# Near products over blocks of 16 tokens, split between VectorE and GpSimd, in a recurrent attention with a feed-forward

## The chip, the cores and the metric

The kernel runs on one core of a Trainium2 chip, in one launch. The metric is the device time in microseconds (us) of an execution; the time before is the median of 6 runs. The profiles are of one execution each. The engines are called by their names in the profile: PE (TensorE, matmuls; PEld are its weight loads), DVE (VectorE), ACT (ScalarE), POOL (GpSimd) and SP (SyncE, which here only issues DMAs).

## The reference

A recurrence over 768 tokens for 4 x 8 heads of 48 channels, then a feed-forward over all 3072 tokens with weights of 384 x 2048 and 2048 x 384:

```python
for t in range(S):
    kt, vt, rt, wt = (k[:, :, t], v[:, :, t], r[:, :, t], w[:, :, t])
    cur = np.einsum('bhd,bhe->bhde', u[None] * kt, vt)
    y[:, :, t] = np.einsum('bhd,bhde->bhe', rt, state + cur)
    state = wt[:, :, :, None] * state + np.einsum('bhd,bhe->bhde', kt, vt)
...
h = x @ w_in
sp = np.maximum(h, 0.0) + np.log1p(np.exp(-np.abs(h)))
g = h * erf(sp)
return (g @ w_out).astype(np.float32)
```

For one head, the weight with which token t reads token s before it is the sum over channels of r[t] k[s] times the product of w over the tokens between them; for s = t it is the sum of r u k. All of it is computed in fp32.

## The kernel before

**Steps.** The work is cut into 12 steps, s = 0 to 11. A step is a stretch of 128 tokens for 2 of the 4 batches, that is 16 heads; even steps hold one pair of batches, odd steps the other. The text counts them from one as well: the fifth step is s = 4. Each step has an attention (`attend`, L350) and a feed-forward of 256 tokens in two halves: `hidden` (L520, 8 pieces of 6 matmuls on L547, then softplus, erf and a product, L529, L532, L536) and `project` (L559, 8 pieces of 4 matmuls on L568). While step s runs its attention, the hidden part of step s - 1 and the projection of step s - 3 run as filling between the attention's parts.

**Levels.** Within a half of 64 tokens the weights between tokens are made by doubling. At level l the pairs are those whose blocks of 2^(l-1) tokens are neighbours in one block of 2^l. PE multiplies r with k (L390, 32 matmuls of 64 x 64 into the tile pp, each of two passes, so 64 instructions in the profile), and the part that belongs to the level is taken over into the tile own (copy_predicated with a mask, L409, on DVE; level 6 by a copy on ACT, L416). Before that DVE scales r and k in place by the totals of w (`scale`, L231), so that the next level's products have the decay in them: the matmuls of level l + 1 wait for the scale of level l. The totals, products of w over 2, 4, ... tokens, are made on POOL (L306, six instructions a step, tile tot_sb).

**Near tokens.** From s = 4 on (`DIRECT`), levels 1 to 3 aren't made by PE. The weights within blocks of `NEAR` = 8 tokens are made directly: r, k and w of the step are loaded a second time with tokens as rows (`load_rows`, L150), and for each distance n from 0 to 7 POOL multiplies k by one more w (L295) and by r (L289, L292, L296). DVE sums each over the 48 channels (L324, tile sums), the sums go to memory and come back with another shape (L330, L332, tiles by_blocks and by_tokens), and one product with a block mask (L342) spreads them over own. In these steps PE makes levels 4, 5 and 6.

**Order.** The kernel writes the order of each engine's queue by hand; every engine works through its queue in order. `prepare(s + 1)` (L235) is a generator: the attention of step s takes one stretch of it at a time, by `next(following)` at L420 and after the transposes (L455), and what is left after the states. Its first stretch has the near products and totals. `place(n)` (L654) is called at each level and at two further points; it runs what is due of softplus, erf and product (`advance`) and then pieces of projection or hidden (`beside`). From s = 4 on these are 4, 4, 3, 3 and 2 pieces in the five places. SP's queue has all loads and stores: behind a step come the three transfers into xT (L512), then the loads for the step after next (`load_step`, `load_rows`), the two stores of o (L578), by_blocks and by_tokens.

**Rest of a step.** After the levels: matmuls from own (L435), transposes of k (L446), new states (L464; DVE L476 and L484, POOL L452 and L480), matmuls from the states into y (L498), and y goes over ACT and DMAs into xT, the feed-forward's input. In the first four steps weights are also converted (L187 to L203), and all six levels run on PE.

The line that says when a stretch of the preparation is taken is

```python
            if level > (NEAR_LOG if s >= DIRECT - 1 else 1):
                next(following, None)
            place(level - 1)
```

Of the kernel before, what the change touches and what calls it, by code (L numbers as in the profile page):

```python
# [11 lines left out]
FP32 = mybir.dt.float32  # L12
# [21 lines left out]


DIRECT = 4
NEAR_LOG = 3
NEAR = 1 << NEAR_LOG
LOG = 6
MASKED = 5  # L40
# [2 lines left out]
def view(ap, offset, dims):  # L43

    return bass.AP(ap.tensor, ap.offset + offset, [ap.ap[0], *dims])
# [12 lines left out]
def kernel(  # L58
# [28 lines left out]
    assert n_steps == SPC * n_pairs and NP == KT + 1 == 4 and NG == 2 and P // NEAR * NH // 2 == P  # L87
# [23 lines left out]
    first = const.tile([P, HC], FP32, name="first")  # L111
    block_sb = const.tile([P, HC], FP32, name="block_sb")

    sums = const.tile([P, NEAR, 2, NEAR], FP32, name="sums")
    u_row = const.tile([P, 2 * D], FP32, name="u_row")
# [110 lines left out]
    def scale(s, level):  # L226

        in_t, tots = loaded[s][0], ready[s][1]
        half, nb = 1 << (level - 1), JP * C >> level
        halves = view(in_t[:, 0:2], half, [[JP * C - half, 2], [2 * half, nb], [1, half]])  # L230
        nc.vector.tensor_mul(  # L231
            halves, halves, view(tots[level - 1], 0, [[1, 2], [2, nb], [0, half]])
        )

    def prepare(s):  # L235


        in_t = loaded[s][0]
        if s < DIRECT:
            rk1 = att.tile([P, 2, JP, C], FP32, name="rk1", bufs=1)  # L240
            parts = 1 if s else NJ
            def multiply_u(i, x):
                n = slice(i * JP // parts, (i + 1) * JP // parts)
                with_u, plain = (
                    [
                        t[:, x, n].rearrange("p n (t two) -> p n t two", two=2)[..., one]
                        for t in (rk1, in_t)
                    ]
                    for one in (x, 1 - x)
                )  # L250
# [12 lines left out]
                nc.scalar.copy(plain[0], plain[1])  # L263

            if s < 2:
                for i in range(parts):
                    for x in range(2):
                        multiply_u(i, x)
                yield
            else:  # L270
                yield
                yield
                multiply_u(0, 0)
        if s >= DIRECT:
# [4 lines left out]
            room = [front[:].rearrange("p x n t -> p (x n t)")] + [  # L279
                back[:].rearrange("p x n two -> p (x n two)").bitcast(FP32)  # L280
            ]
            terms = []
            for n in range(NEAR):
                if n in (0, 3):
                    free, used = room.pop(0), 0
                size = (NEAR - n) * 2 * D
                terms.append(free[:, used : used + size].rearrange("p (t n) -> p t n", n=2 * D))
                used += size
            nc.gpsimd.tensor_mul(  # L289
                terms[0], k, u_row[:, None, :].to_broadcast([P, NEAR, 2 * D])  # L290
            )
            nc.gpsimd.tensor_mul(terms[0], terms[0], r)  # L292
            for n in range(1, NEAR):
                if n > 1:
                    nc.gpsimd.tensor_mul(k[:, : NEAR - n], k[:, : NEAR - n], w[:, n - 1 : NEAR - 1])  # L295
                nc.gpsimd.tensor_mul(terms[n], r[:, n:], k[:, : NEAR - n])  # L296

        tots, tot = [], in_t[:, 2].rearrange("p n t -> p (n t)")
        tot_sb = att.tile([P, JP * (C - NC)], FP32, name="tot_sb")
        used = 0  # L300
        for level in range(1, LOG + 1):
            tots.append(tot)
            nb = JP * C >> level
            new = tot_sb[:, used : used + nb]
            pair = tot.rearrange("p (n two) -> p n two", two=2)
            nc.gpsimd.tensor_mul(new, pair[:, :, 0], pair[:, :, 1])  # L306
            tot = new
            used += nb
            if level == 2 and s < DIRECT:
                yield  # L310
        if s < DIRECT:
            ready[s] = rk1, tots, tot
            yield
            if s >= 2:
                yield
                multiply_u(0, 1)
            return

        own = att.tile([P, NH, HC], FP32, name="own")
        ready[s] = own, tots, tot  # L320
        yield
        yield
        for n in range(NEAR):
            nc.vector.tensor_reduce(  # L324
                out=view(sums[:], n, [[2 * NEAR + 1, NEAR - n], [NEAR, 2]]),
                in_=terms[n].rearrange("p t (n d) -> p t n d", d=D),
                axis=mybir.AxisListType.X, op=ALU.add,
            )
        by_blocks = dram.tile([P, NEAR, 2 * NEAR], FP32, name="by_blocks")
        nc.sync.dma_start(out=by_blocks[:], in_=sums[:].rearrange("p s n t -> p s (n t)"))  # L330
        by_tokens = att.tile([P, NH, NEAR], FP32, name="by_tokens", bufs=1)
        nc.sync.dma_start(  # L332
            out=by_tokens[:].rearrange("p (g n) t -> p g (n t)", n=2),
            in_=by_blocks[:].rearrange("(g b) s n -> (b s) g n", g=NH // 2),
        )
# [13 lines left out]

    def attend(s, xT, place, behind):  # L350
# [29 lines left out]
        for level in range(NEAR_LOG + 1 if s >= DIRECT else 1, LOG + 1):  # L380
# [213 lines left out]
    def beside(s, k):  # L594


        kind, of, pieces = (projs, s - 3, 2) if k < 4 else (hids, s - 1, 2)
        if s >= DIRECT:
            kind, of = (projs, s - 3) if k < 2 else (hids, s - 1)
            pieces = (4, 4, 3, 3, 2)[k]  # L600
        if s in ALONE:
            kind, of, pieces = hids, s - 1, 1
        if not 0 <= of < n_steps:
# [3 lines left out]
        for _ in range(pieces):  # L607
            next(kind[of])


    CONVERT = (
# [13 lines left out]
    with tc.manual_schedule(  # L625
# [19 lines left out]
        for s in range(n_steps):  # L645
            xTs[s] = xs.tile([P, KT, UNIT], FP32, name="xT")
            places = iter(range(8))

            def convert_at(n):
                if s < len(CONVERT) and n < len(CONVERT[s]):  # L650
                    for what in CONVERT[s][n]:
                        conversion.send(what)

            def place(n):  # L654
                if s in ALONE:
                    convert_at(n)
                    advance(ALONE[s][n])
                else:
                    advance()
                    convert_at(n)  # L660
                beside(s, next(places))

            attend(s, xTs[s], place, lambda: convert_at(LOG + 2))
            if s + 2 < n_steps:
                load_step(s + 2)
                if s + 2 >= DIRECT:
                    load_rows(s + 2)
        for k in range(15):
            advance()
            beside(n_steps + k // 5, k % 5)  # L670


def level_masks():
# [94 lines left out]
```

## Time and profile before

| | |
|---|---|
| median of 6 runs | 637.38 us (637.2 to 638.08) |
| the profiled execution | 637.2 us, of it 635.4 us span |
| granted PE clock | 1.000 |
| DVE, L231, scales, 72 of 128 x 1024 | 100.9 us busy |
| DVE, L536, h products, 48 of 128 x 1024 | 80.1 us busy, 1708 ns each |
| DVE, L324, reduces, 64 of 16 down to 2 sums | 38.2 us busy |
| POOL, L289 to L296, near products, 120 | 134.4 us busy |
| POOL, L306, totals, 72 | 66.8 us busy |

Busy time is what the instructions of a group took from start to end, so it has in it what an instruction lost to others after it had started. An engine's idle time costs nothing by itself; it does where the engine is the one that the end waits for. In rows of a timeline the first number is the start in the span, the second the time from the first start to the last end of a run of equal instructions, and a bracket at the end is the idle time before it and who ended it.

How the twelve steps lie: the fourth step (s = 3) goes from 105.7 to 158.4 us, the eight late steps (s = 4 to 11) follow at 48.8 us each until 549.2 us, and then the last projections run until the end.

### The profile page before, as it was taken

Reading aid. Unit: us, or ns where it says so; the run is one execution under the profiler, and the core shown is the slowest. Engines: PE = TensorE matmul, PEld = TensorE weight load, DVE = VectorE, ACT = ScalarE, POOL = GpSimd, SP = SyncE. Lnnn points to the kernel's source line nnn. Section 1 sums busy time; section 2 is a strip of 40 time slices with the busy share of each in tenths; the row PEclk is TensorE's granted clock in tenths of the full one; section 3 lists DMA queues with packets and bytes.
Section 4 is the critical chain, followed back from the end, with each engine's and each line's share of the span. In section 5 each row is a group of like instructions: output and inputs, shape, how many; then the busy total and the mean of one; then the engine's idle time right before and its main releaser. Section 6 shows DMA issues by size and latency. Waiting matters only on the chain.

```text
span 635.4 us, 16193 instructions
## 1 busy us (share of the span) xinstructions
PE 622.4 (98%) x7338; PEld 458.2 (72%) x7338; DVE 307.6 (48%) x311; ACT 301.1 (47%) x374; POOL 276.0 (43%) x240
## 2 busy tenths in 40 slices
PE   8889999999999999999999999999999999999997
PEld 7567787678678678668668668768768758768654
DVE  4588597577336276266265365366446322011110
ACT  2537778756424544544534524624614625634520
POOL 4338175495195196097097087088079100000000
PEclk9999999999999999999999999999999999999999
DMA  8366371500500500500510410420330000000000
GB/s 329 130 238 201 140 257 52 204 15 10 207 25 10 207 26 9 206 26 10 187 44 10 178 55 9 152 80 9 104 127 11 8 13 14 7 23 3 1 25 25
DMA packets 24628, 53.84 MB, mean 85 GB/s; under 512 B 11376, under 2 KB 16752, under 8 KB 23152
## 3 DMA queue, kind: packets, MB, share of 16 engines
q1 hardware_dynamic: 23408, 52.23, 22.8%
q8 instruction: 57, 0.93, 0.6%
q10 hardware_dynamic: 1152, 0.59, 0.4%
q14 instruction: 11, 0.09, 0.1%
HBM read 46.39 MB, written 5.24 MB: 81 GB/s over the span
## 4 chain that ended last, share of the span: by engine, by line
PE 91%; DMA 3%; DVE 2%; ACT 1%; issue 1%; POOL 0%; SPq 0%; ACTq 0%
PE m L568 40%; PE m L547 38%; PE pp L390 6%; DMA in<-in_rkw 3%; PE y L435 2%; PE pp L446 2%; PE y L498 2%; PE pp L464 2%; DVE in L231 1%; DVE own L409 1%; ACT own L416 0%; POOL tot_sb L306 0%; DMA xT<-y 0%; DVE pp L196 0%; ACT pp L187 0%
## 5 line engine op out<-in xcount | busy, mean ns | idle before, releaser
L547 PE MATMUL m<-xT,w_in_sb 128*128 128x256 f32 x1152 | 260.1, 382 | 0.6 <-DMA xT<-y 0.3
L568 PE MATMUL m<-w_out_sb,h 128*128 128x384 f32 x768 | 253.5, 489 | 0.0
L547 PEld LDWEIGHTS m<-xT,w_in_sb 128*128 128x128 f32 x1152 | 214.6, 190 | 33.1 <-issue 1.6
L568 PEld LDWEIGHTS m<-w_out_sb,h 128*128 128x128 f32 x768 | 144.2, 190 | 97.4
L231 DVE TENSOR_TENSOR in<-in,tot_sb 128x1024 f32<-128x1024 f32 x60 | 81.7, 1362 | 153.8 <-PE pp L390 151.0
L536 DVE TENSOR_TENSOR h<-h,sp 128x1024 f32<-128x1024 f32 x48 | 80.1, 1708 | 67.7 <-ACT sp L532 67.7
L554 ACT COPY h<-m 128x512 f32<-128x512 f32 x96 | 56.1, 584 | 104.3 <-PE m L547 104.1
L577 ACT COPY o<-m 128x384 f32<-128x384 f32 x24 | 11.5, 479 | 148.3 <-PE m L568 136.5
L289 POOL TENSOR_TENSOR rk<-words,u_row 128x768 f32<-128x768 f32 x8 | 16.5, 2057 | 124.6 <-DMA words<-in_rk_rows 124.6
L306 POOL TENSOR_TENSOR tot_sb<-tot_sb 128x256 f32<-128x256 f32 (+4 forms) x60 | 54.3, 905 | 4.5
L390 PEld LDWEIGHTS pp<-in 48*64 48x64 f32 (+1 forms) x2816 | 41.0, 127 | 20.6 <-issue 17.6
L295 POOL TENSOR_TENSOR words<-words,rest 128x576 f32<-128x576 f32 (+5 forms) x48 | 51.6, 1075 | 3.8
L390 PE MATMUL pp<-in 48*64 48x64 f32 (+1 forms) x2816 | 46.5, 214 | 4.3 <-DVE own L409 2.2
L532 ACT ACTIVATE sp<-sp 128x2048 f32<-128x2048 f32 x24 | 45.8, 1910 | 0.3
L529 ACT ACTIVATE sp<-h 128x2048 f32<-128x2048 f32 x24 | 45.8, 1910 | 0.3
L532 ACT ACT_TABLE_LOAD x24 | 30.8, 1283 | 20.2 <-issue 19.9
L296 POOL TENSOR_TENSOR words<-words 128x480 f32<-128x480 f32 (+4 forms) x40 | 34.4, 861 | 3.1
L529 ACT ACT_TABLE_LOAD x24 | 30.8, 1283 | 3.3 <-issue 2.9
L296 POOL TENSOR_TENSOR rk<-words 128x672 f32<-128x672 f32 (+1 forms) x16 | 31.9, 1993 | 0.6
L324 DVE TENSOR_REDUCE sums<-words 128x10 f32<-128x480 f32 (+4 forms) x40 | 17.8, 452 | 26.3 <-POOL words L296 25.9
L203 POOL TENSOR_TENSOR w_out_sb<-w_out_sb,rest 128x768 int32<-128x768 int32 x8 | 18.1, 2267 | 27.5 <-DVE w_out_sb L199 27.5
L476 DVE TENSOR_TENSOR middle<-faded,pp 48x384 f32<-48x384 f32 x20 | 11.0, 552 | 33.2 <-PE pp L464 32.9
(57 smaller groups left out, 426.7 us busy)
## 6 DMA issues: line engine op xcount, KB each, us to landing
in<-in_rkw SPq DMA_DIRECT2D x11, 1536.0 KB, 6.6
words<-in_moe_w_in SPq DMA_DIRECT2D x8, 768.0 KB, 5.7
words<-in_moe_w_out SPq DMA_DIRECT2D x8, 768.0 KB, 4.5
words<-in_rk_rows SPq DMA_DIRECT2D x8, 768.0 KB, 8.3
v<-in_v SPq DMA_DIRECT2D x12, 384.0 KB, 6.9
out<-o SPq DMA_DIRECT2D x24, 192.0 KB, 1.9
rest<-in_w_rows SPq DMA_DIRECT2D x8, 384.0 KB, 8.9
in<-in_rkw SPq DMA_DIRECT2D x2, 512.0 KB, 4.5
```

Source lines behind the costliest of these rows:

```text
L203: nc.gpsimd.tensor_tensor(out=into, in0=into, in1=rest[:], op=ALU.add)
L231: nc.vector.tensor_mul(halves, halves, view(tots[level - 1], 0, [[1, 2], [2, nb], [0, half]]))
L295: nc.gpsimd.tensor_mul(k[:, : NEAR - n], k[:, : NEAR - n], w[:, n - 1 : NEAR - 1])
L296: nc.gpsimd.tensor_mul(terms[n], r[:, n:], k[:, : NEAR - n])
L306: nc.gpsimd.tensor_mul(new, pair[:, :, 0], pair[:, :, 1])
L390: nc.tensor.matmul(pp[s0 : s0 + m, e, n, :m], lhsT=rk[rows(e), 1, n, s0 : s0 + m], rhs=rk[rows(e), 0, n, t0 : t0 + m], start=True, stop=True,)
L529: nc.scalar.activation(held[0][:], h[:], AF.Softplus)
L532: nc.scalar.activation(held[0][:], held[0][:], AF.Erf)
L536: nc.vector.tensor_mul(h[:, part], h[:, part], held[0][:, part])
L547: nc.tensor.matmul(ps[:, ff, :], lhsT=w_in_sb[:, g * FG + f + ff, kk * P : (kk + 1) * P], rhs=xT[:, kk, :], start=kk == 0, stop=kk == KT - 1,)
L554: nc.scalar.copy(h[:, f : f + FT, :], ps[:])
L568: nc.tensor.matmul(ps[j][:], lhsT=gs[g][:, f, j * C : (j + 1) * C], rhs=w_out_sb[:, g * FG + f, :], start=g + f == 0, stop=g == NG - 1 and ...
```

## The change

Blocks of 16 tokens in place of 8 (`NEAR_LOG` 3 to 4), so that in the late steps PE makes levels 5 and 6 alone. The rows are laid out anew (16 tokens x 48 channels for one head in each row instead of 8 x 96 for two), of the same size. The near products of distances 0 to 4 (`NEARER`) and their sums are written for DVE, those of distances 5 to 15 for POOL, with the sums on DVE two stretches later. The totals stand ahead of them in POOL's queue. Products 5 to 15 are written where products 0 to 4 stood. The sums that go to memory and back are twice as many.

For the fifth step (s = 4) the first stretch of its preparation is taken at level 3 of the fourth step (s = 3), the next at level 6; from the fifth step on it is taken at level 5. In the late steps the filling is laid out by a string for each of four places: A is what is due of softplus, erf and product, P a piece of projection, H one of hidden. The rows for the step after next are asked for at level 6 instead of behind the step. y3 has one buffer.

```diff
-NEAR_LOG = 3
+NEAR_LOG = 4
+NEARER = 5
...
+            for room, distances in (
+                (front, range(1, 4)), (back, (0, 4)), (front, range(5, 9)), (back, range(9, NEAR))
+            ):
+                used = 0
+                for n in distances:
+                    size = (NEAR - n) * D
+                    terms[n] = room[:, used : used + size].rearrange("p (t d) -> p t d", d=D)
+                    used += size
+
+            def sum_up(n):
+                nc.vector.tensor_reduce(
+                    out=view(sums[:], n, [[NEAR + 1, NEAR - n]]), in_=terms[n],
+                    axis=mybir.AxisListType.X, op=ALU.add,
+                )
+
+            def carry(engine, n):
+
+                if 1 < n < NEAR:
+                    engine.tensor_mul(
+                        k[:, : NEAR - n], k[:, : NEAR - n], w[:, n - 1 : NEAR - 1]
+                    )
...
         own = att.tile([P, NH, HC], FP32, name="own")
         ready[s] = own, tots, tot
+        nc.vector.tensor_mul(terms[0], k, u_row[:, None, :].to_broadcast([P, NEAR, D]))
+        nc.vector.tensor_mul(terms[0], terms[0], r)
+        for n in range(1, NEARER):
+            nc.vector.tensor_mul(terms[n], r[:, n:], k[:, : NEAR - n])
+            carry(nc.vector, n + 1)
+        for n in range(NEARER):
+            sum_up(n)
+        for n in range(NEARER, NEAR):
+            nc.gpsimd.tensor_mul(terms[n], r[:, n:], k[:, : NEAR - n])
+            carry(nc.gpsimd, n + 1)
         yield
         yield
...
+        for n in range(NEARER, NEAR):
+            sum_up(n)
+        by_blocks = dram.tile([P, NEAR, NEAR], FP32, name="by_blocks")
+        nc.sync.dma_start(out=by_blocks[:], in_=sums[:])
         by_tokens = att.tile([P, NH, NEAR], FP32, name="by_tokens", bufs=1)
...
+        for level in range(1, NEAR_LOG):
+            scale(s, level)
         yield
-        scale(s, 1)
-        scale(s, 2)
-        yield
-        scale(s, 3)
+        scale(s, NEAR_LOG)
...
-            if level > (NEAR_LOG if s >= DIRECT - 1 else 1):
+            if level in (3, LOG) if s == DIRECT - 1 else level > (NEAR_LOG if s >= DIRECT else 1):
                 next(following, None)
             place(level - 1)
...
-        y3 = att.tile([P, UNIT], FP32, name="y3")
+        y3 = att.tile([P, UNIT], FP32, name="y3", bufs=1)
...
+    def in_order(s, k):
+        for what in ("APPPAPP", "APPPHH", "AHHH", "AHHH")[k]:
+            if what == "A":
+                advance()
+            elif what == "P":
+                piece(projs, s - 3)
+            else:
+                piece(hids, s - 1)
...
             def place(n):
+                if n == LOG - 1 and DIRECT - 1 <= s < n_steps - 2:
+                    load_rows(s + 2)
+                if s >= DIRECT:
+                    in_order(s, next(places))
+                    return
```

More of the change, by code (lines that the diff above doesn't have):

```diff
@@ L86 @@
     assert C == P == NC * HC and HC == 1 << LOG and NE == 2 and D <= EP and NP * NE * D == DM == KT * P
-    assert n_steps == SPC * n_pairs and NP == KT + 1 == 4 and NG == 2 and P // NEAR * NH // 2 == P
+    assert n_steps == SPC * n_pairs and NP == KT + 1 == 4 and NG == 2 and P // NEAR * NH == P
     const = ctx.enter_context(tc.tile_pool(name="const", bufs=1))
@@ L112 @@
     block_sb = const.tile([P, HC], FP32, name="block_sb")
-    sums = const.tile([P, NEAR, 2, NEAR], FP32, name="sums")
-    u_row = const.tile([P, 2 * D], FP32, name="u_row")
+    sums = const.tile([P, NEAR, NEAR], FP32, name="sums")
+    u_row = const.tile([P, D], FP32, name="u_row")
     w_in_sb = const.tile([P, NT, DM], FP32, name="w_in_sb")
@@ L278, in prepare @@
             back = wide.tile([P, 2, DM, 2], I32, name="words", bufs=3)
[L279 to L296, printed above, removed]
+            front = front[:].rearrange("p x n t -> p (x n t)")
+            back = back[:].rearrange("p x n two -> p (x n two)").bitcast(FP32)
+            terms = {}
+            for room, distances in (
[16 more added lines that the diff above has]
+                    )
         tots, tot = [], in_t[:, 2].rearrange("p n t -> p (n t)")
@@ L320, in prepare @@
         ready[s] = own, tots, tot
+        nc.vector.tensor_mul(terms[0], k, u_row[:, None, :].to_broadcast([P, NEAR, D]))
[8 more added lines that the diff above has]
+            carry(nc.gpsimd, n + 1)
         yield
         yield
[L323 to L330, printed above, removed]
+        for n in range(NEARER, NEAR):
+            sum_up(n)
+        by_blocks = dram.tile([P, NEAR, NEAR], FP32, name="by_blocks")
+        nc.sync.dma_start(out=by_blocks[:], in_=sums[:])
         by_tokens = att.tile([P, NH, NEAR], FP32, name="by_tokens", bufs=1)
         nc.sync.dma_start(
-            out=by_tokens[:].rearrange("p (g n) t -> p g (n t)", n=2),
-            in_=by_blocks[:].rearrange("(g b) s n -> (b s) g n", g=NH // 2),
-        )
+            out=by_tokens[:], in_=by_blocks[:].rearrange("(g b) s t -> (b s) g t", g=NH)
+        )
+        for level in range(1, NEAR_LOG):
+            scale(s, level)
         yield
-        scale(s, 1)
-        scale(s, 2)
-        yield
-        scale(s, 3)
+        scale(s, NEAR_LOG)
         nb = HC // NEAR
@@ L597, in beside, with piece @@
         kind, of, pieces = (projs, s - 3, 2) if k < 4 else (hids, s - 1, 2)
-        if s >= DIRECT:
-            kind, of = (projs, s - 3) if k < 2 else (hids, s - 1)
-            pieces = (4, 4, 3, 3, 2)[k]
         if s in ALONE:
             kind, of, pieces = hids, s - 1, 1
+        for _ in range(pieces):
+            piece(kind, of)
+    def piece(kind, of):
         if not 0 <= of < n_steps:
@@ L606, in beside @@
             kind[of] = hidden(xTs[of], gated[of]) if kind is hids else project(of, gated[of])
-        for _ in range(pieces):
-            next(kind[of])
+        next(kind[of])
+    def in_order(s, k):
[6 more added lines that the diff above has]
+                piece(hids, s - 1)
     CONVERT = (
@@ L665 @@
                 load_step(s + 2)
-                if s + 2 >= DIRECT:
+                if s + 2 == DIRECT:
                     load_rows(s + 2)
-        for k in range(15):
-            advance()
-            beside(n_steps + k // 5, k % 5)
+        for k in range(12):
+            in_order(n_steps + k // 4, k % 4)
 def level_masks():
@@ L711, in by_blocks @@
     def by_blocks(x):
-        x = x.reshape(B // NJ, NJ, NP // 2, 2, 2, n_pairs, P // NEAR, NEAR, D).transpose(
-            5, 0, 4, 1, 2, 6, 7, 3, 8
+        x = x.reshape(B // NJ, NJ, NP, 2, n_pairs, P // NEAR, NEAR, D).transpose(
+            4, 0, 3, 1, 2, 5, 6, 7
         )
@@ L718 @@
     u_rows = np.broadcast_to(
-        u.reshape(NP // 2, 2, 2, D).transpose(2, 0, 1, 3)[:, None, :, None],
-        (2, NJ, NP // 2, P // NEAR, 2, D),
+        u.reshape(NP, 2, D).transpose(1, 0, 2)[:, None, :, None], (2, NJ, NP, P // NEAR, D)
     )
@@ L753 @@
         "in_w_rows": by_blocks(w),
-        "in_u_rows": np.ascontiguousarray(u_rows).reshape(P, 2 * D),
+        "in_u_rows": np.ascontiguousarray(u_rows).reshape(P, D),
     }
```

## The prediction

> **What bounds the kernel now.** I read the page's first part, then the chain of waits, then the timelines of the engines in one late step and in the fourth step, where the diff moves work.
>
> ```profile
> span 635.4 us, 16193 instructions
> PE 622.4 (98%) x7338; PEld 458.2 (72%) x7338; DVE 307.6 (48%) x311; ACT 301.1 (47%) x374; POOL 276.0 (43%) x240
> PE 91%; DMA 3%; DVE 2%; ACT 1%; issue 1%; POOL 0%; SPq 0%; ACTq 0%
> ```
>
> TensorE (PE) is busy through 98% of the span and makes 91% of the chain. Whatever leaves its queue shortens the time, and whatever makes it idle lengthens it. The chain in order of time (start, duration, engine, tile, line) shows a late step:
>
> ```profile
> 256.25 0.93 PE pp L390 x64
> 257.18 10.52 PE m L568 x32
> 267.70 1.09 PE pp L390 x64
> 268.79 10.52 PE m L568 x32
> 279.31 0.69 PE pp L390 x50
> ```
>
> These are the products of levels 4, 5 and 6 with the projection between them. The next step's first product starts at 305.09, so a step takes 48.84 us, all of it PE. The time outside the span is 637.2 - 635.4 = 1.8 us; the profiled 637.2 us is 0.2 under the median of 637.38, so the sum is made against 637.2.
>
> Two timelines show how VectorE (DVE) and GpSimd (POOL) stand to each other. First DVE, then POOL:
>
> ```profile
> 270.61 4.99 DVE L536 TENSOR_TENSOR h<-h,sp 128x1024 f32<-128x1024 f32 x2
> ...
> 514.77 2.35 DVE L536 TENSOR_TENSOR h<-h,sp 128x1024 f32<-128x1024 f32 x2
> ```
>
> ```profile
> 271.84 2.68 POOL L292 TENSOR_TENSOR rk<-rk,words 128x768 f32<-128x768 f32 x1
> 274.47 2.59 POOL L296 TENSOR_TENSOR rk<-words 128x672 f32<-128x672 f32 x1
> 277.14 1.41 POOL L295 TENSOR_TENSOR words<-words,rest 128x576 f32<-128x576 f32 x1
> ```
>
> The same two DVE products take 2.35 us alone and 4.99 us beside POOL's products; POOL's product of 768 takes 2.68 us here and 1.81 us in the fourth step, where DVE is idle. The ends interlock: they take turns, one instruction each. Reduces, and operations with an operand in PSUM, take no turn (the three reduces at 281.18 take 2.37 us while POOL's 480 and 384 take 1.21 and 1.01 us, their times alone). Up to now this costs nothing, because PE's queue is long enough to hide it.
>
> **Part 1, removed: level 4's products in steps 5 to 12.** Of the two wide groups the one between projections goes, 1.09 us. Eight steps: -8.7 us; a step becomes 48.84 - 1.09 = 47.75 us. Bounds by the rows: 0.93 x 8 = 7.4 and 1.16 x 8 = 9.3. Level 4's copy_predicated (0.71) leaves DVE; its scale stays.
>
> **Part 2, added on DVE: ten products and five reduces per step.** A product of 1024 takes 1.23 us, so about 0.16 + n/960 us, and 0.03 more where it needs the one before. The ten hold 768+768+720+672+672+624+624+576+576+528 = 6528 elements: 6.8 + 10 x 0.18 = 8.6 us. Reduces: 2016 elements took 2.37 us, so 3360 take 3.95 us. In a late step these 12.6 us lie beside 10.5 us and more of projection.
>
> **Part 3, POOL.** 21 products of 5808 elements instead of 15 of 6240. Rows: 96 elements 0.39, 288 0.80, 480 1.21, 576 1.41 us, so 0.185 + n x 0.00212, and 0.08 between two: about 17.6 us, against about 17.2 before. But they begin later: the 6 totals (L306) now come first, distance 5 needs DVE's last carry, and it is written where distances 1 and 2 stand, so it waits for two reduces (1.85 us).
>
> **Part 4, the fourth step.** For the fifth step's sums the DVE work stands in the queue after level 3's scale and copy, ahead of level 4's scale, which level 5's products need. DVE, then POOL, then PE there:
>
> ```profile
> 119.77 1.23 DVE L231 TENSOR_TENSOR in<-in,tot_sb 128x1024 f32<-128x1024 f32 x1
> 120.92 0.70 DVE L409 COPY_PREDICATED own<-mask_sb,pp 128x512 f32<-128x512 int32 x1
> 126.22 1.23 DVE L231 TENSOR_TENSOR in<-in,tot_sb 128x1024 f32<-128x1024 f32 x1 [4.61 <-PE pp L390]
> ```
>
> ```profile
> 119.95 2.72 POOL L203 TENSOR_TENSOR w_out_sb<-w_out_sb,rest 128x768 int32<-128x768 int32 x1 [8.03 <-DVE w_out_sb L199]
> ```
>
> ```profile
> 126.09 5.43 PE L568 MATMUL m<-w_out_sb,h 128*128 128x384 f32 x16
> 131.44 1.16 PE L390 MATMUL pp<-in 48*64 48x64 f32 x64
> ```
>
> DVE is free at 121.62. It waits for L203 until 122.67 (1.05), makes ten products (8.6) and gives POOL six turns for the totals (1.04 for the first and 3.11 for the other five alone, at 20.11: 4.1). That is 135.4. Five reduces end at 139.3, a turn of POOL's costs about 0.6, level 4's scale 1.2: 141.1. PE has run out of projection at 131.44, so it idles 9.7 us. Without any turns it is 121.62 + 8.6 + 3.95 + 1.2 = 135.4, an idle of 4.0: the lower bound.
>
> A second chain ends later still. POOL's products begin at 135.4 + 1.85 = 137.25, take 17.6, and give turns to seven DVE products (three scales, four of L536; 7 x 1.15 = 8.05): 162.9. Behind the last of them DVE has a reduce (0.25), a wait for the faded state (0.65), three scales (3.45), the middle state (1.15), the next state with POOL's part (2.05) and level 4's scale (1.2): 8.75, so 171.65. The fifth step's level 5 can't begin before; the step began at 158.58. So part 4 costs 13.1 us, which takes in the 9.7. After its stop PE needs, by the old rows, 158.4 - 131.44 = 27.0 us to the step's end: 141.1 + 27.0 = 168.1, so 3.5 us of PE's lateness are free there.
>
> No row shows what PE's clock does after such a stop: its longest waits here are under 2 us, and the granted clock is 1.00 in every stretch. The Trainium skill, "TensorE: Matmul & The Clock Gate", section "What's actually happening", speaks against the change: after an idle window of about 3.4 us the clock is halved, until about 3.4 us of work have passed. By it an estimated 1.7 us would be lost after the stop, and the sum would not change, since 3.5 us are free.
>
> **Part 5, the late steps: does it fit in 47.75 us?** From the start of level 5's products: DVE free at 2.96 (259.21 - 256.25); ten products 8.6; turns for the first two totals 1.8 (the next inputs land at about 9.5 to 10: issued 2.9 to 3.9 after the step's start, 6.3 to 7.3 to landing); two reduces 1.85; POOL 17.6; turns for two of L536 and a scale 3.45; then the 8.75 of above and two more of L536 (2.35). Sum 47.4: it fits by 0.4. But where a step starts late against the end of the last, as the fifth does by some 3 us, the inputs land early, all totals take turns ahead of DVE's products (4.1 instead of 1.8), and the chain is 49.7 at most: an idle of about 1.5, then 0.9, then 0.3, and about 0.8 in all for the uneven landings after. Together 3.5 us; bounds 0 (no turns) and 9 (1.3 in each of seven steps).
>
> **Costed at nothing:** by_blocks and by_tokens double (64 KB took 1.5 and 2.2 us; at most 7.4), and must land in the 8.5 us that the fourth step has between the last reduce and the own product (10.9 later); uncovered, they would cost what they exceed it by, in each of eight steps. SP's queue takes the next rows ahead of the out stores; their room was freed a step earlier, so the stores aren't held. ScalarE's erf now stands ahead of the copy of o: late by 2 us, hidden by two pieces of projection (5.3 us). y3 with one buffer waits for a transfer that is a step old.
>
> **Sum:** 635.4 - 8.7 + 13.1 + 3.5 = 643.3, and 1.8 around it: 645.1, so 645 us.
>
> **Rivals.** (a) Faster: the turns cost almost nothing, as now for the products of levels; then part 4 is its lower bound and part 5 nothing: 637.2 - 8.7 + 4.0 = 632.5. For it: PE is the only bound now. Against it: 4.99 against 2.35 us. It decides if DVE's block in the fourth step ends before about 136. (b) Only the fourth step hurts and the late ones fit: 637.2 - 8.7 + 13.1 = 641.6. For it: the margin of 0.4. (c) POOL and DVE set the pace of every step, with idles of 1.3 us: 637.2 - 8.7 + 13.1 + 9 = 650.6. For it: a chain within 1% of the step. Against it: an idle once taken lets the inputs land early for only part of the chain.
>
> **How the numbers follow.** Forecast (643 to 648) 0.45; (b) 0.21; (c) 0.15; (a) 0.12; a fourth step that costs 8 to 10 with late steps that fit, which is no change, 0.05; the rest 0.02, slower. Faster by over 0.2% (about 1.3 us, what a measurement of this kernel can tell from no change): 0.12; within: 0.05; slower: 0.83. The range reaches below (b) and to the edge of (c): 638 to 650.
>
> **What would show it.** PE idle of 8 to 10 us in the fourth step behind the level 4 projection, released by DVE's scale; the fifth step's first product 10 to 14 us later than 158.58; steps of 47.75 us late in the span; DVE products of 768 with 1.5 us and more there instead of 0.96. If the fourth step's stop is under 5 us, part 4 is wrong; if late steps are above 48.84, part 5 is.

## The result and the profile after

The changed kernel takes 635.63 us (median of 21 executions, 634.69 to 637.55) against 637.3 us before (42 executions): a ratio of 0.9974, 95% interval 0.9968 to 0.998. It is 0.26% faster, where 645 us and slower had been forecast. The profiled execution took 635.33 us, of it 633.5 us span, against 635.4 us span before; the difference to be explained is 1.9 us.

The page of the kernel after, its first part, the row of the granted clock and the chain by engine:

```profile
span 633.5 us, 15381 instructions
PE 612.8 (97%) x6826; PEld 451.3 (71%) x6826; DVE 402.7 (64%) x447; ACT 301.2 (48%) x374; POOL 259.2 (41%) x288
...
PEclk9999999979999999999999999999999999999999
...
PE 83%; DVE 7%; POOL 4%; issue 3%; ACT 2%; DMA 1%; SPq 0%; DVEq 0%; POOLq 0%; ACTq 0%
```

PE has 9.6 us less work, and the time falls by 1.9. The chain now runs through DVE and POOL for a stretch, and one slice of the clock has a 7. Both belong to the fourth step. First its DVE queue, in order of time, from level 3's scale on (the last line is level 4's scale):

```profile
119.78 1.23 DVE L232 TENSOR_TENSOR in<-in,tot_sb 128x1024 f32<-128x1024 f32 x1
120.92 0.71 DVE L422 COPY_PREDICATED own<-mask_sb,pp 128x512 f32<-128x512 int32 x1
121.52 1.98 DVE L330 TENSOR_TENSOR words<-words,u_row 128x768 f32<-128x768 f32 x1
123.53 1.68 DVE L331 TENSOR_TENSOR words<-words 128x768 f32<-128x768 f32 x1
125.14 1.31 DVE L333 TENSOR_TENSOR rk<-words 128x720 f32<-128x720 f32 x1
126.48 0.94 DVE L302 TENSOR_TENSOR words<-words,rest 128x672 f32<-128x672 f32 x1
...
131.62 0.71 DVE L302 TENSOR_TENSOR words<-words,rest 128x528 f32<-128x528 f32 x1
...
136.04 1.77 DVE L232 TENSOR_TENSOR in<-in,tot_sb 128x1024 f32<-128x1024 f32 x1
```

and POOL beside it, with the totals, and the first and the last of the near products:

```profile
122.64 1.76 POOL L315 TENSOR_TENSOR tot_sb<-in 128x512 f32<-128x512 f32 x1
124.47 4.76 POOL L315 TENSOR_TENSOR tot_sb<-tot_sb 128x256 f32<-128x256 f32 x5
134.14 1.32 POOL L338 TENSOR_TENSOR rk<-words 128x528 f32<-128x528 f32 x1 [4.91 <-issue]
...
157.70 0.28 POOL L338 TENSOR_TENSOR words<-words 128x48 f32<-128x48 f32 x1
```

PE in the same stretch: its stop before level 5, the hidden pieces behind it, and the fifth step's first product:

```profile
137.87 1.98 PE L403 MATMUL pp<-in 48*64 48x64 f32 x64 [6.35 <-DVE in L232]
139.78 6.24 PE L560 MATMUL m<-xT,w_in_sb 128*128 128x256 f32 x24
...
166.79 1.16 PE L403 MATMUL pp<-in 48*64 48x64 f32 x64 [0.17 <-DVE in L232]
```

The fifth step begins at 166.79 instead of 158.58 in the chain: the fourth step costs 8.2 us more. Behind that, the late steps, in the chain in order of time:

```profile
214.57 0.93 PE pp L403 x64
215.50 13.10 PE m L581 x40
228.60 0.69 PE pp L403 x50
...
262.12 0.93 PE pp L403 x64
```

A step takes 262.12 - 214.57 = 47.55 us, where it took 48.84, and no wait stands in it. Eight of them give 10.3 us back, 0.2 less in the first. So: +8.2 - 10.1 = -1.9.

### The profile page after: what moved, and what is told of

Its sections match the earlier page's. It is cut to its first block, busy times and chain, and to the rows that moved or that the text cites. A ratio compares the mean times of both kernels' runs of the same rounds, so it can differ in the third digit from the quotient of the medians.

```text
span 633.5 us, 15381 instructions
## 1 busy us (share of the span) xinstructions
PE 612.8 (97%) x6826; PEld 451.3 (71%) x6826; DVE 402.7 (64%) x447; ACT 301.2 (48%) x374; POOL 259.2 (41%) x288
## 4 chain that ended last, share of the span: by engine, by line
PE 83%; DVE 7%; POOL 4%; issue 3%; ACT 2%; DMA 1%; SPq 0%; DVEq 0%; POOLq 0%; ACTq 0%
PE m L581 37%; PE m L560 34%; PE pp L403 5%; DVE in L232 2%; PE y L448 2%; PE pp L459 2%; POOL words L302 2%; PE y L511 2%; PE pp L477 2%; POOL words L338 1%; DVE own L422 1%; POOL rk L338 1%; DMA in<-in_rkw 1%; DVE sums L294 1%; DVE words L302 1%
## 5 line engine op out<-in xcount | busy, mean ns | idle before, releaser
L302 POOL TENSOR_TENSOR words<-words,rest 128x480 f32<-128x480 f32 (+4 forms) x80 | 69.3, 866 | 6.3
L294 DVE TENSOR_REDUCE sums<-words 128x16 f32<-128x768 f32 (+8 forms) x72 | 33.1, 462 | 47.6 <-POOL words L338 47.6
L315 POOL TENSOR_TENSOR tot_sb<-in 128x512 f32<-128x512 f32 x12 | 15.3, 1278 | 112.6 <-DMA in<-in_rkw 112.6
L338 POOL TENSOR_TENSOR rk<-words 128x528 f32<-128x528 f32 (+3 forms) x32 | 51.7, 1616 | 7.8 <-issue 4.9
L403 PEld LDWEIGHTS pp<-in 48*64 48x64 f32 (+1 forms) x2304 | 33.6, 128 | 23.3 <-issue 10.1
L403 PE MATMUL pp<-in 48*64 48x64 f32 (+1 forms) x2304 | 38.1, 215 | 11.1 <-DVE in L232 7.3
L294 DVE TENSOR_REDUCE sums<-rk 128x15 f32<-128x720 f32 (+6 forms) x56 | 37.2, 713 | 8.8 <-POOL rk L338 8.8
L338 POOL TENSOR_TENSOR words<-words 128x336 f32<-128x336 f32 (+6 forms) x56 | 34.9, 624 | 4.4
L315 POOL TENSOR_TENSOR tot_sb<-tot_sb 128x256 f32<-128x256 f32 (+4 forms) x60 | 32.3, 538 | 4.5
L429 ACT COPY own<-pp 32x512 f32<-32x512 f32 x24 | 13.8, 574 | 40.1 <-PE pp L403 39.8
```

The source lines that it names most:

```text
L294: nc.vector.tensor_reduce(out=view(sums[:], n, [[NEAR + 1, NEAR - n]]), in_=terms[n], axis=mybir.AxisListType.X, op=ALU.add,)
L302: engine.tensor_mul(k[:, : NEAR - n], k[:, : NEAR - n], w[:, n - 1 : NEAR - 1])
L403: nc.tensor.matmul(pp[s0 : s0 + m, e, n, :m], lhsT=rk[rows(e), 1, n, s0 : s0 + m], rhs=rk[rows(e), 0, n, t0 : t0 + m], start=True, stop=True,)
```

## The experiments

The question was what the 8.2 us are. Theory 1: two ends meet at the fifth step's start. PE comes late out of its stop, and the chain over DVE and POOL to that step's level 4 scale ends at the same moment (the wait left is 0.17 us). Theory 2: PE's stop alone. Theory 3: the chain alone. Kernels 1 to 4 ran together on one chip, with the kernel before at 637.48 us; executions of one kernel spread over up to 3 us (634.69 to 637.55 for the changed one), so the fifth step's start in the profile is the finer measure. Starts are given against the moment at which DVE takes up the fourth step's level 3 scale, since the first four steps differ by up to 1.5 us from the changed kernel's: 166.79 - 119.78 = 47.0 us in the changed kernel.

**1. PE kept busy in its stop.**

```diff
+            if level == 5 and s == DIRECT - 1:
+                stay_warm(6)
             pp = products([P, NE, JP, HC])
```

> The changed kernel with six more matmuls on TensorE (into an unused PSUM tile) between the fourth step's last projection piece and its level 5 products, where TensorE sat idle for 6.35 us and the granted clock fell to 0.50 in the next 3.4 us. Theory 1 (two ends meet: TensorE's late end of the fourth step at 166.6 us, and the DVE and POOL chain to the fifth step's level 4 scale at 166.75): the clock stays at 1.00, level 5 takes 1.16 us instead of 1.98 and the next hidden pieces 5.45 instead of 6.24, TensorE's fourth step ends 1.6 us earlier, and the fifth step still begins at 166.8: time unchanged within 0.3 us, with a wait of some 1.8 us in place of 0.17 before the fifth step. Theory 2 (TensorE's stop alone sets the end): 1.6 us less than the changed kernel.

635.85 us (10 executions). PE's timeline in this kernel, from the added matmuls on:

```profile
131.78 5.31 PE L389 MATMUL m<-in,ident 128*128 128x512 f32 x12
138.29 1.16 PE L405 MATMUL pp<-in 48*64 48x64 f32 x64 [1.20 <-DVE in L232]
139.38 5.45 PE L562 MATMUL m<-xT,w_in_sb 128*128 128x256 f32 x24
...
167.24 1.16 PE L405 MATMUL pp<-in 48*64 48x64 f32 x64 [1.81 <-DVE in L232]
```

The slow matmuls are gone (1.16 for 1.98, 5.45 for 6.24), PE is ready 1.6 us earlier, and it waits 1.81 us in place of 0.17. The start is at 47.03: unchanged. Theory 2 falls. What the halved clock takes was time that PE had to spare.

**2. The chain taken away.** All four scales of the fifth step come ahead of the sums that wait for POOL, and are left out where they stood:

```diff
+        if s == DIRECT:
+            for level in range(1, NEAR_LOG + 1):
+                scale(s, level)
         for n in range(NEARER, NEAR):
             sum_up(n)
```

> The changed kernel with the fifth step's four scales (levels 1 to 4) ahead of the eleven sums that wait for POOL. It takes the DVE and POOL chain away from the fifth step's start. Theory 1 (two ends meet): TensorE's own end of the fourth step, 166.6 us, is left as the bound; 0.2 us less than the changed kernel, no more, and the wait before the fifth step is gone. Theory 3 (the DVE and POOL chain alone sets the end): the fifth step begins 3 us and more earlier, so 3 us less.

636.02 us (7 executions). The wait before the fifth step is gone, and it begins at 47.43, not 3 us earlier: PE itself is no earlier. It is 0.4 later than in the changed kernel because the hidden pieces behind the stop, of the same length, took 7.02 us in this execution (6.24 there). Theory 3 falls.

**3. PE's stop shortened.** The fifth step's sums of distances 2 to 4 wait until level 4's scale and copy are done:

```diff
         for n in range(NEARER):
+            if s == DIRECT and n == 2:
+                yield
             sum_up(n)
...
-            if level in (3, LOG) if s == DIRECT - 1 else ...
+            if level in (3, 4, LOG) if s == DIRECT - 1 else ...
```

> The changed kernel with the fifth step's sums of distances 2 to 4 behind the fourth step's level 4 scale and copy. TensorE's idle in the fourth step falls from 6.35 to about 4.1 us. Theory 1 (two ends meet): the fifth step begins at 166.7 all the same, because POOL's products start and end as before; time unchanged within 0.3 us, and a wait of about 2 us stands before the fifth step. Theory 2 (TensorE's stop alone): 2.2 us less.

The fifth step's first product, in PE's timeline:

```profile
165.76 1.20 PE L405 MATMUL pp<-in 48*64 48x64 f32 x64 [1.26 <-DVE in L232]
```

The stop falls from 6.35 to 3.66 us, and the start stays at 47.01 to the hundredth, with a wait of 1.26 us in front of it, as theory 1 says. The wait is shorter than the 2 us expected because the slow stretch behind the stop cost more here: level 5 and the hidden pieces take 1.99 and 7.84 us for 1.16 and 5.45, 3.2 us in place of 1.6. The profiled execution took 634.33 us, about 1 us less than the changed kernel's, and that lies in the first steps (level 3's scale at 118.75 instead of 119.78). The median of the ten was 637.79, 2 us above the changed kernel; experiments 9 and 10 take that up.

**4. Both edits.**

> Both of the last two edits together. Theory 1 (two ends meet): only now does the time fall, by 2.0 to 2.5 us against the changed kernel (633.3 to 633.6 us), the fifth step beginning at about 164.4. Theory 2 (TensorE's stop alone): the same 2.2 us as the sums alone gave. Theory 3 (the chain alone): as the scales alone gave.

```profile
164.65 1.11 PE L410 MATMUL pp<-in 48*64 48x64 f32 x64
```

633.47 us (4 executions; ratio to the kernel before 0.9935, 0.992 to 0.9949). The fifth step begins at 44.79, 2.2 us earlier, and no wait stands before it. Neither edit alone gave that: theory 1 stands.

| | fourth step's stop | wait before the fifth step | its start | median |
|---|---|---|---|---|
| changed kernel | 6.35 | 0.17 | 47.01 | 635.63 |
| 1, PE busy | 1.20 after 5.31 us of added work | 1.81 | 47.03 | 635.85 |
| 2, scales first | 6.34 | none | 47.43 | 636.02 |
| 3, sums later | 3.66 | 1.26 | 47.01 | 637.79 |
| 4, both | 3.67, then 0.68 | none | 44.79 | 633.47 |
| 6, at level 5 | 3.90, then 5.33 | 2.23 | 54.24 | 644.89 |
| 8, reordered | 0.46 | none | 39.16 | 627.42 |
| 9, as 3 | 3.66 | 1.65 | 47.01 | 636.98 |
| 10, as 3, PE busy | 1.10 after 2.74 us of added work, then 2.38 | 2.17 | 47.16 | 636.01 |

**5. How much room a late step has.** The add of the middle state three times more in the late steps:

```diff
-                nc.vector.tensor_add(middle[rows(e)], faded[0][rows(e)], ps[rows(e), 0, :, :D])
+                for _ in range(4 if s >= DIRECT else 1):
+                    nc.vector.tensor_add(
+                        middle[rows(e)], faded[0][rows(e)], ps[rows(e), 0, :, :D]
+                    )
```

> The changed kernel with the add of the middle state (two instructions on DVE with an operand in PSUM) repeated three more times in each late step: 3.4 us more on the DVE and POOL chain in front of the next step's level 4 scale, in the seven late steps that prepare a step. Reading of the changed kernel's profile: that scale ends at 355.16 us and the next step's first product begins at 357.21, a margin of 2.05 us in each late step; then 1.3 us too much a step, 7 to 10 us in all more than the changed kernel. If the margin were 0.4 us, as the prediction had it, 3.0 us a step, about 21 us. If the late steps hung on TensorE alone, nothing.

648.87 us (4 executions), 13.2 more than the changed kernel, where 7 to 10 had been expected. The late steps take about 49.5 us (49.1 to 50.1), 1.95 more, but for the last that prepares a step (47.58; no next state stands in its chain). The eight adds take 4.64 us in place of 1.13, so 3.5 more. The chain grows by a little more: from a step's first scale to the next step's level 4 scale it takes 46.96 us (367.26 to 414.22) instead of 43.27 (310.66 to 353.93). The other 0.2 us go with the totals, whose inputs now land 7.5 us after that first scale instead of 8.9, so that they meet more of DVE's products. The room was thus 3.7 - 1.95 = 1.75 us, near the 2.05 that I read off the profile and far from the 0.4 of the prediction. The late steps are safe, but not by much.

**6. The fifth step's preparation at level 5**, where the late steps take theirs:

```diff
-            if level in (3, LOG) if s == DIRECT - 1 else ...
+            if level in (5, LOG) if s == DIRECT - 1 else ...
```

> The changed kernel with the first stretch of the fifth step's preparation taken at level 5 of the fourth step instead of level 3 (the second at level 6 in both). Theory 1 (two ends meet): TensorE's stop gets shorter (about 4.7 us, before the transposes), but DVE's products end at 144 instead of 132.3, POOL's at about 167 instead of 158, and the fifth step begins at about 176 instead of 166.8: 9 us more than the changed kernel, about 644.6 us. Theory 2 (TensorE's stop alone sets the end): 2 to 3 us less than the changed kernel.

644.89 us (4 executions). PE's timeline of this kernel has three waits:

```profile
148.77 1.97 PE L459 MATMUL pp<-ident,in 128*128 128x128 f32 x8 [3.90 <-DVE in L232]
...
170.34 1.68 PE L511 MATMUL y<-in,middle 48*48 48x64 f32 x32 [5.33 <-DVE middle L489]
174.25 1.99 PE L403 MATMUL pp<-in 48*64 48x64 f32 x64 [2.23 <-DVE in L232]
```

The first is shorter than the changed kernel's stop, and the others are the chain: POOL's products end at 165.4 instead of 158, the states wait for them, and the fifth step begins 7.2 us later. Its first product takes 1.99 us, so the clock is down there too, with nothing to hide it, and the fifth step takes 49.4 us (174.25 to 223.64) instead of 47.6; the 9.3 us of the medians are these two, 7.2 and 1.8. Level 3 was the better place because it starts the chain 13 us earlier, although it stops PE.

**7. What a turn costs.** Behind the last instruction, 8 equal instructions each on DVE and on POOL start together, in seven groups (one execution):

```diff
+        for vector, gpsimd in (
+            ("multiply", None), (None, 192), ("multiply", 192), (None, "pairs"),
+            ("multiply", "pairs"), ("reduce", 192), ("multiply", 768),
+        ):
```

> The changed kernel with a probe behind its last instruction, when DVE and POOL have nothing else: groups of 8 equal instructions on DVE and on POOL that start together. It leaves nothing out; its time is longer by the probe. Theory T (in a turn DVE waits for POOL's whole instruction, as the prediction had it): 8 DVE products of 768 alone about 7.0 us; beside 8 POOL products of 192 (0.59 us each alone) 11.8; beside 8 POOL products of 64 pairs (about 0.45 each) 10.6. Theory R (DVE waits only for the part that grows with the elements, 2.12 ns each): 10.3 beside the 192, 8.1 beside the 64 pairs. Both: 8 reduces of 768 take the same time beside POOL as alone, 6.9 us; 8 POOL products of 768 beside 8 of DVE take the sum, about 21 us.

DVE's timeline (the products of 768, alone, beside 192, beside 64 pairs; the reduces beside 192; the products beside 768), then POOL's (192 alone and beside, 64 pairs alone and beside, 192 beside reduces, 768 beside products):

```profile
608.20 7.91 DVE L721 TENSOR_TENSOR words<-words,rest 128x768 f32<-128x768 f32 x8
...
623.47 9.81 DVE L721 TENSOR_TENSOR words<-words,rest 128x768 f32<-128x768 f32 x8
...
638.70 7.91 DVE L721 TENSOR_TENSOR words<-words,rest 128x768 f32<-128x768 f32 x8
...
647.79 7.87 DVE L724 TENSOR_REDUCE words<-rest 128x16 f32<-128x768 f32 x8
...
656.75 18.27 DVE L721 TENSOR_TENSOR words<-words,rest 128x768 f32<-128x768 f32 x8
```

```profile
617.18 5.26 POOL L733 TENSOR_TENSOR rk<-words,rest 128x192 f32<-128x192 f32 x8 [120.58 <-DVE rest L718]
623.51 10.21 POOL L733 TENSOR_TENSOR rk<-words,rest 128x192 f32<-128x192 f32 x8 [1.07 <-DVE rest L718]
634.79 2.88 POOL L731 TENSOR_TENSOR rk<-rest 128x64 f32<-128x64 f32 x8 [1.07 <-DVE rest L718]
638.75 8.02 POOL L731 TENSOR_TENSOR rk<-rest 128x64 f32<-128x64 f32 x8 [1.07 <-DVE rest L718]
647.84 5.26 POOL L733 TENSOR_TENSOR rk<-words,rest 128x192 f32<-128x192 f32 x8 [1.07 <-DVE rest L718]
656.80 19.89 POOL L733 TENSOR_TENSOR rk<-words,rest 128x768 f32<-128x768 f32 x8 [3.71 <-DVE rest L718]
```

DVE is first in each group, so its eight products meet seven of POOL's. Beside POOL's products of 192, DVE loses 9.81 - 7.91 = 1.9 us in seven turns, 0.27 each (its products take 1.23 instead of 0.96), where POOL's instruction takes 0.59 alone. Beside those of 768 it loses 10.36, 1.48 each, where POOL's takes 1.81 (in the fourth step before, with DVE idle). Both are POOL's time less 0.32 to 0.33. Beside the 64 pairs, 0.29 us each, DVE loses nothing, while POOL goes from 2.88 to 8.02. POOL loses in the same way: 10.21 - 5.26 and 8.02 - 2.88 in eight turns are 0.62 and 0.64 each, DVE's 0.96 less 0.32 to 0.34. So in these groups each engine waits only for what is over about a third of a microsecond of the other's instruction, and POOL's instructions that are shorter cost DVE nothing. Theory T falls; theory R, whose figures were 10.3 and 8.1, is nearer, but prices 192 elements at 0.41 us a turn where 0.27 was measured. Reduces cost nothing on either side, as both had it: POOL takes 5.26 us as alone, and a reduce of 768 about 0.95, as in the changed kernel's fourth step at 132.25, where POOL is idle.

**8. A kernel without both ends.** What waits for POOL goes behind everything that the next step's first product needs:

```diff
         for n in range(1, NEARER):
+            if s == DIRECT and n == 4:
+                yield
             nc.vector.tensor_mul(terms[n], r[:, n:], k[:, : NEAR - n])
             carry(nc.vector, n + 1)
+        yield
         for n in range(NEARER):
             sum_up(n)
         for n in range(NEARER, NEAR):
             nc.gpsimd.tensor_mul(terms[n], r[:, n:], k[:, : NEAR - n])
             carry(nc.gpsimd, n + 1)
         yield
+        for level in range(1, NEAR_LOG + 1):
+            scale(s, level)
         yield
         for n in range(NEARER, NEAR):
             sum_up(n)
...
             scale(s, level)
+            if s >= DIRECT and level == NEAR_LOG + 1:
+                spread(s, own)
...
-            if level in (3, LOG) if s == DIRECT - 1 else ...
+            if level in (3, 4, 5) if s == DIRECT - 1 else ...
...
-            nc.gpsimd.tensor_mul(
+            (nc.vector if s >= DIRECT - 1 else nc.gpsimd).tensor_mul(
                 faded[0][:], S[:], ends[:, :, 0:1].to_broadcast([P, JP, D])
```

`spread` is the product into own, moved; the scales are left out where they stood, and the product into faded[1] changes engine as well.

> A kernel built on theory 1: nothing that waits for POOL's near products stands ahead of what the next step's first product needs. For the fifth step eight of DVE's ten products stay at level 3, two go to level 4, the sums and POOL's products to level 5; in all late steps the sums of distances 0 to 4 and POOL's products come one stretch later, the four scales come ahead of the other sums, these sums behind the states, the product into own behind the next step's level 5 scale, and the products with the faded states on DVE. By theory 1 the fourth step's stop falls to about 0.7 us, the fifth step begins at 159 to 160 instead of 166.8, and the late steps keep 47.55 us: 627.7 us, 7 to 8 less than the changed kernel. By theory 2 (TensorE's stop alone) 7 us less as well. If the late steps get new waits, from POOL running later and beside more of DVE's products, they show before a step's first product or before the states' part, and the time is above 630.

627.42 us (4 executions; ratio to the kernel before 0.9844, 0.9829 to 0.9859). PE's timeline in the fourth step and at the fifth step's start:

```profile
132.53 1.16 PE L410 MATMUL pp<-in 48*64 48x64 f32 x64 [0.46 <-DVE in L232]
133.63 5.45 PE L569 MATMUL m<-xT,w_in_sb 128*128 128x256 f32 x24
...
159.49 1.11 PE L410 MATMUL pp<-in 48*64 48x64 f32 x64
```

The stop is 0.46 us, the clock stays up, the fifth step begins without a wait (at 39.16, where the kernel before has 158.40 - 119.77 = 38.63), and the late steps keep their 47.55 us. The gain that the change has in it comes out: 10 us, 1.6%.

**9 and 10. Why experiment 3 ran slower than its profile.** The same kernel again, and one with three more matmuls (`stay_warm(3)`) in its stop:

> The kernel of e3_sums_later once more, unchanged: there the profiled execution took 634.3 us, as theory 1 said, but the median of ten was 637.8, with times up to 638.8. If that belongs to the kernel, the median is again 2 us and more above the changed kernel's 635.6, and a profiled execution of such a time shows where the rest goes: the granted clock halved for longer than the 3.4 us after the stop of 3.7 us, or a later step's wait. If it was chance, the median is 634.3 to 635.6.

> The kernel of e3_sums_later with three more matmuls on TensorE in the stop that is left (3.7 us), so that TensorE isn't idle there for more than about 1 us. If the halved clock after the stop makes the spread of e3_sums_later, the times now lie together at 634.5 to 635.6 us and the granted clock stays at 1.00; if the spread has another cause, it is there again. By theory 1 the fifth step begins no earlier than in e3_sums_later in either case.

Experiment 9 has a median of 636.98 us (10 executions, 635.42 to 639.49), and its profiled execution took 637.1. The fifth step begins at 47.01 again, but what follows is slow. The windows of this kernel (stretch, its length, busy time of PE, PE's loads, DVE, ACT and POOL with their counts, then the granted clock) and its PE timeline:

```profile
150.00:166.00 16.00, 15.21 (x252) 12.74 (x250) 11.85 (x20) 10.95 (x13) 8.80 (x14) 1.00 0.11 18
166.00:172.00 6.00, 5.15 (x72) 3.20 (x72) 5.79 (x7) 3.86 (x5) 0.00 (x0) 0.72 0.50 158
```

```profile
166.85 1.16 PE L405 MATMUL pp<-in 48*64 48x64 f32 x64 [1.65 <-DVE in L232]
167.94 14.86 PE L583 MATMUL m<-w_out_sb,h 128*128 128x384 f32 x40
```

The clock falls a second time, behind a wait of 1.65 us, and five pieces of projection take 14.86 us instead of the 13.17 of a late step. That is 1.7 us, and by as much this execution's span, 635.3 us, is above the changed kernel's 633.5 (1.8). In experiment 3's profiled execution the wait was 1.26 us and the clock stayed at 1.00. So part of the time that the fourth step's stop gave up came back as a second slow stretch, this time with nothing to hide it. Experiment 10 shows the same: the clock stays at 1.00 through the fourth step, six of ten executions lie at 635.15 to 636.25 us, and four at 637.23 to 640.17; the profiled one is the slowest, with a wait of 2.17 us before the fifth step, its projection at 15.51 us behind it, and a start that was 1.5 us late before the fourth step. My expectation that the spread would go was wrong, since I had filled the first stop and left the second. That this second fall makes up all of experiment 3's median isn't shown. Of its ten executions the mean granted clock is on record: the six at 0.989 to 0.992 took 636.62 to 638.77 us, the four at 0.994 and 0.995 took 634.33 to 637.16. So more time at the halved clock goes with the longer times, but two executions at 0.995 still lie 2.8 us apart, and the first four steps vary as well.

## Why the prediction was wrong, point by point

- **Part 1** was right in kind and short in size: -8.7 us forecast, 8 x (48.84 - 47.55) = -10.3 measured. Level 4's products gave the 1.09. The other 0.2 came from the new string of filling: two pieces of hidden now follow projection directly, and the eight pieces take 5.18 + 7.77 + 7.97 = 20.92 us instead of 7.97 + 7.77 + 5.38 = 21.12.
- **Part 2** was right: with POOL idle, the ten products of a late step run from 312.52 to 321.80, 9.3 us, of it 0.7 for one turn, where 8.6 us had been forecast without turns; the five reduces of the fourth step take 3.9 us.
- **Part 4 failed in the price of its turns.** I let DVE wait for the whole of each of the six totals, 4.1 us, so that its products would end at 122.67 + 8.6 + 4.1 = 135.4. They ended at 132.33: the turns cost 1.1 us. One of the 3 us too much was a misread row. The 3.11 us that I took for the five smaller totals alone have a scale of DVE inside them, in the kernel before (POOL, then DVE):

```profile
21.23 3.11 POOL L306 TENSOR_TENSOR tot_sb<-tot_sb 128x256 f32<-128x256 f32 x5
22.34 1.23 DVE L231 TENSOR_TENSOR in<-in,tot_sb 128x1024 f32<-128x1024 f32 x1 [1.59 <-POOL tot_sb L306]
```

  Experiment 6 shows them with DVE idle:

```profile
123.99 2.07 POOL L315 TENSOR_TENSOR tot_sb<-tot_sb 128x256 f32<-128x256 f32 x5
```

  The other 2 us are the part of an instruction for which DVE doesn't wait, as experiment 7 measured it: the six totals take 1.03, 0.61, 0.40 and three times under 0.3 us alone (experiment 6), and less 0.33 each, but never below nothing, that is 0.70 + 0.28 + 0.07 = 1.05 us.
- The same part was missing in POOL's stretch, 134.14 to 157.98, 23.8 us where 25.65 had been forecast: seven turns at about 0.86 us instead of 1.15. (Part 3's own formula gives 17.8 us for POOL's products, not 17.6.) The 8.75 us behind it were 166.79 - 157.98 = 8.8. So the chain ended at 166.79 instead of 171.65, 3.1 us by the totals and 1.8 by POOL's turns, and part 4 cost 8.2 instead of 13.1 us.
- That PE's stop and this chain would run side by side, with time to spare for a halved clock, was right. The stop was 6.35 instead of 9.7 us, between the 8 to 10 that were to show the forecast and the 5 below which part 4 was to be wrong. The windows of the changed kernel behind it, with the clock in the third column from the end:

```profile
131.40:137.80 6.40, 0.12 (x1) 0.00 (x0) 6.37 (x9) 3.67 (x3) 3.50 (x3) 0.75 0.58 216
137.80:141.20 3.40, 3.33 (x67) 2.97 (x68) 3.40 (x4) 0.00 (x0) 3.24 (x3) 0.50 0.00 1
141.20:144.60 3.40, 3.40 (x17) 2.98 (x16) 3.40 (x3) 0.59 (x1) 3.32 (x2) 0.97 0.00 0
```

  The mean of 0.75 says that the clock fell inside the stop, and it stays at 0.50 for the first 3.4 us of the work behind it. That costs 0.8 us twice, 1.6 us, near the 1.7 that the Trainium skill's "TensorE: Matmul & The Clock Gate", section "What's actually happening", let me estimate. The nearness is partly luck: behind the same stop it cost 2.4 us in experiment 2 and behind a shorter one 3.2 in experiment 3, and the granted clock is down for 6.8 us in all three. Experiment 1 shows that the 1.6 us were free here.
- **Part 5 failed**: 3.5 us of idle time forecast, none seen. A late step's first total and its level 4 scale for the next step, which ends the chain:

```profile
319.60 1.64 POOL L315 TENSOR_TENSOR tot_sb<-in 128x512 f32<-128x512 f32 x1 [14.18 <-DMA in<-in_rkw]
353.93 1.23 DVE L232 TENSOR_TENSOR in<-in,tot_sb 128x1024 f32<-128x1024 f32 x1
```

  The chain ends at 355.16, 45.5 us after the step's start, not 47.4; the totals delay DVE by about 0.7 us instead of 1.8, and three turns cost POOL 0.9 us less in sum. So this is part 4's wrong price again. And the late start of the fifth step, from which the forecast idles followed, wasn't there: PE's own end was as late as the chain's, so the next inputs were asked for no earlier. (Experiment 5, where the steps do start late, shows the early landing that part 5 feared, at 0.2 us a step.)
- **The sign** came from all of these together. Part 4 at its measured size leaves 645.1 - 4.9 = 640.2 us, still slower. Part 5's 3.5 and part 1's 1.6 do the rest, less the 0.2 of the first late step: 635.3 us, as profiled.
- **The rivals.** Rival (a) had the sign and the wrong cause: its price of 4.0 us needs turns that cost nothing, and the measured cost was 8.2. What was to decide for it, a block on DVE that ends before about 136, stood on the edge: the fifth reduce ended at 136.13. The case that happened, a fourth step at 8 us with late steps that fit, stood in the text as no change, at 5%; with part 1 at its measured size it is 0.26% faster.

## What to carry to other kernels

When two engines take turns, measure what a turn costs the one that waits: here it was the other's duration less a third of a microsecond, and the smallest instructions didn't delay DVE at all. When a row is taken as an instruction's time alone, look at the other engine's timeline first. When the bounding engine stops, look for a second chain that ends at the same moment: each of two single repairs then shows nothing, and only both together show what there is to gain. What waits for the slower helper goes behind everything that the next product needs.

## What the runs showed of the hardware that had not been expected

- In the probe (experiment 7), where both operands lie in SBUF, a DVE product waits for a POOL product by POOL's time alone less 0.32 to 0.33 us (1.48 of 1.81, 0.27 of 0.59, 0 of 0.29), and a POOL product for DVE's by 0.62 to 0.64 of 0.96.
- Behind a stop of 6.35 us the granted clock was at 0.50 for 3.4 us of work, and the cost of such a stretch was 1.6, 2.4 and 3.2 us in three kernels (experiments 2 and 3 the last two). It fell too behind waits of 1.65 and 2.17 us at a step's end (five pieces at 14.86 and 15.51 us for 13.17), and not behind waits of 1.26 and 1.81 us at the same place, nor behind one of 2.38 us in experiment 10's fourth step. In experiment 5 it fell behind 1.71 and 1.83 us, and not behind 1.34 and 1.72. What decides it isn't shown.
